# A linear-attention recurrence whose instruction order is a plan made in the kernel, on one core of a Trainium2

## The chip, the cores and the metric

The kernel runs on one core of a Trainium2 chip. The core has a matrix engine (TensorE, PE; its weight loads are listed apart as PEld), a vector engine (VectorE, DVE), an activation engine (ScalarE, ACT), a general engine (GpSimd, POOL) and SyncE (SP), which here only issues transfers (DMAs). Each engine takes its instructions strictly in the order in which they stand in its program and waits at each one until its inputs are there and its output buffer is free; the order of each engine is fixed when the kernel is built. The metric is the time of one execution in microseconds (us).

## The reference

Two parts follow each other: a recurrence over 768 time steps for 4 sequences of 8 heads with head size 40, and a mixture of 8 experts over its 3072 outputs.

```python
for t in range(S):
    y[:, :, t] = np.einsum('bhd,bhde->bhe', rt, state)
    Sa = np.einsum('bhde,bhe->bhd', state, at)
    state_decay = state * wt[:, :, None, :] - np.einsum('bhd,bhe->bhde', Sa, bt)
    state = state_decay + np.einsum('bhd,bhe->bhde', vt, kt)
...
logits = x @ w_gate
logits = logits - logits.max()
P = np.exp(logits)
for _ in range(8):
    P /= P.sum(1, keepdims=True) + 1e-09
    P /= P.sum(0, keepdims=True) + 1e-09
    P *= N / E
for e in range(E):
    h = np.maximum(x @ w1[e], 0.0)
    ye = h @ w2[e]
    out += P[:, e:e + 1] * ye
```

## The kernel before

The recurrence (function `attention`, lines 29 to 385) is cut into 12 chunks of 64 steps. Within a chunk the steps are solved as a triangular system, so that matrix products take the place of the loop over steps; between chunks a state of 40 by 40 per head is carried. A unit is one chunk of one sequence: 12 x 4 = 48 units, numbered chunk by chunk, and each unit holds 8 heads in 4 pairs.

Four kinds of work make up the recurrence.

- `prep(c, b)` needs only the inputs of unit (c, b). SP loads `inp`; VectorE scans the decays into q (L114), takes a reciprocal (L118) and scans g (L122); GpSimd (VectorE for the first units) multiplies kb and the two halves of ab (L133, L139, L140) and copies cc (L138); TensorE makes ll (L145) and the transposes kt (L153); VectorE masks ll into sx (L155), ScalarE copies the rest into sx and bb and stores lt to a DRAM buffer ld. What prep makes (sx, bb, g, cc) stays in one of 17 sets of buffers until the unit has been recurred, so preparations can run up to 17 units ahead.
- The inversion runs for two chunks at once, 128 small triangular blocks of 32 by 32, one in each partition. Eight transfers bring them from ld into lu (L342), 42 VectorE instructions build the inverse in un (L170 and L173 column by column, then products and reductions of 512, 1024 and 2048 elements, L179 and L182), one copy (L331) transposes it, and it goes out to the DRAM buffers ud and nd.
- `tload` and `tmat` read ud and nd back and join two blocks of 32 into a triangular factor tt of 64 (gp, L226, and op, L231, on TensorE, copies on ScalarE).
- `recur(c, b)` is the chain of a unit: av (L251), mask f (L252), two products xc (L259), copies x1 and c1 (L265, L266), pu with tt (L270), pm (L272), c2 (L277), ws (L279), then y (L281) to the DRAM buffer xd and z (L292), which, transposed by TensorE (zt, L297), feeds the next chunk of the same sequence. `gate` multiplies y with the gate weights (lp, L307), and a VectorE copy (L312) keeps the logits.

The order is made in two steps. The list `ev` gives each piece of work a time in arbitrary units, and sorting it gives the order in which the code emits instructions:

```python
t = max(t, t0 + P0 + PD * i) if s else -20 + 0.01 * i
ev.append((t, do_prep, (s,) + cb + (i == 0,)))
...
for i, (fn, a) in enumerate(INV):
    ev.append((t + INV_DT * i, fn, (us,) + a))
...
for _, fn, args in sorted(ev, key=lambda x: x[0]):
    fn(*args)
```

A list scheduler with a timing model of its own (`schedule_with_timeline_sim=True`) then takes instructions from that order as their inputs and buffers come free in its model, and so fixes each engine's program. PSUM is divided into three pools of 4, 2 and 2 banks (`ps`, `pq`, `pt`), by kind of product.

The expert part follows from L450 on. Its weights and inputs are prepared on all engines while the last units still run; its buffers lie over those of the recurrence. From block `N_MAN` on its order is written out by hand. The products are `p` (L545) and `op` (L610).

Of the kernel before, what the change touches and what calls it, by code (L numbers as in the profile page):

```python
# [28 lines left out]
def attention(ctx, tc, d, xd, ps, pq, pt, gs, lg):  # L29
# [5 lines left out]
    io = ctx.enter_context(tc.tile_pool(name="a_io", bufs=1))  # L35
    wk = ctx.enter_context(tc.tile_pool(name="a_wk", bufs=2))
    dr = ctx.enter_context(tc.tile_pool(name="a_dr", bufs=2, space=bass.MemoryType.DRAM))

    cst = const.tile([128, 64 + 64 + 104 + 128 + 40 + 260], F32, name="cst")
    nc.sync.dma_start(out=cst, in_=d["cst"])  # L40
# [6 lines left out]
    NTB = 2  # L47
    sx_b, bb_b, g_b, cc_b = ([None] * NSX for _ in range(4))
    raws = {}
    for n in range(NCH * NB - NSX, NCH * NB):  # L50
        i, pool = n % NSX, sets[n - NCH * NB + NSX]
        if i in IN_SETS or i in KB_SETS:
            raw = pool.tile([128, 1508], F32, name=f"st{i}")
            raws[i] = raw
            sx_b[i] = raw[0:R2, 0:832].rearrange("r (p h x) -> r p h x", h=2, x=104)
            bb_b[i] = raw[:, 832:1248].rearrange("r (p x) -> r p x", x=104)
            g_b[i] = raw[0:R2, 1248:1504].rearrange("r (p x) -> r p x", x=64)
            cc_b[i] = raw[0:R2, 1504:1508]
            continue
        sx_b[i] = pool.tile([R2, NP, 2, 104], F32, name=f"sx{i}")  # L60
        bb_b[i] = pool.tile([128, NP, 104], F32, name=f"bb{i}")
        g_b[i] = pool.tile([R2, NP, 64], F32, name=f"g{i}")
        cc_b[i] = pool.tile([R2, NP], F32, name=f"cc{i}")
    tt_b = [const.tile([128, 4 * NP, 128], F32, name=f"tt{i}") for i in range(NTB)]
    td_b = [const.tile([128, 4 * NP, 32], F32, name="td")]
    lg_b = [const.tile([128, 4 * NP, 64], F32, name="lg")]
    ab_b = [pin.tile([R2, NP, 128], F32, name=f"ab{i}") for i in range(2)]
    g1_b = [pin.tile([R2, NP, 64], F32, name=f"g1{i}") for i in range(1)]
    vz_b = [const.tile([R2, NP, 104], F32, name=f"vz{i}") for i in range(5)]
# [8 lines left out]
    for t in g1_b + ab_b:  # L78
        nc.vector.memset(t, 0.0)

    def clear():
        nc.gpsimd.memset(unf, 0.0)
        nc.gpsimd.memset(unf[:, 0:1024:33], 1.0)
        for t in vz_b + c1_b + lg_b:
# [725 lines left out]
```

## Time and profile before

| | us |
|---|---|
| median of 3 runs | 1890.27 |
| lowest and highest run | 1883.09, 1900.79 |
| the profiled execution | 1888.5 |
| its span, first to last instruction | 1886.7 |

The profile shows the profiled execution alone, and its mean granted TensorE clock is 0.945. A row of its groups reads: line, engine, operation, output and input tiles with their sizes, count, then busy time in us and mean duration in ns, then the idle time ahead of them and what ended it. A row of the answers on one line of code has the shortest, the median and the longest duration in ns, and the first and last start. "Records" are the entries of the trace: an fp32 matmul of the program leaves two, a transpose one. TensorE is busy for 94% of the span, VectorE for 74%, ScalarE for 45%, GpSimd for 48%; such shares run over stages with different limits, so the prediction looks at stages.

### The profile page before, as it was taken

The numbers are of one execution on the slowest core, as the hardware profiler recorded it, in microseconds if no ns is written. First come the engines' busy times: TensorE is split into PE (matmuls) and PEld (weight loads), VectorE is DVE, ScalarE is ACT, GpSimd is POOL, SyncE is SP. The second block draws the span as 40 slices with busy tenths as digits, with TensorE's granted clock in tenths as the row PEclk, the third lists the DMA queues.
The fourth block names the chain that finished last, engine by engine and source line by source line (L and its number), as shares of the span: only waits on it lengthen the run. The fifth ranks groups of instructions, "written<-read, shape, count | busy, mean of one in ns | idle before, by whom it ended". The sixth has DMA issues, their size and how long they took to land.

```text
span 1886.7 us, 31821 instructions
## 1 busy us (share of the span) xinstructions
PE 1768.5 (94%) x12035; PEld 1731.1 (92%) x12035; DVE 1395.1 (74%) x2330; ACT 853.9 (45%) x1845; POOL 896.9 (48%) x845
## 2 busy tenths in 40 slices
PE   4478989889998999999999999999999999999999
PEld 4368878789888999999999999999999999999999
DVE  7766768686579877776867777886776767777676
ACT  6346566655553444343433434345343433434342
POOL 6636457562345355371835628004461826537170
PEclk9568889988889999999999999999999999999999
DMA  8567777855732011110201102111110201111011
GB/s 192 102 131 160 137 156 144 176 128 102 164 96 70 32 43 37 37 61 14 73 26 49 55 19 74 55 33 38 37 55 19 73 19 56 37 37 57 17 37 42
DMA packets 187838, 136.26 MB, mean 72 GB/s; under 512 B 155941, under 2 KB 165285, under 8 KB 187685
## 3 DMA queue, kind: packets, MB, share of 16 engines
q1 hardware_dynamic: 184485, 128.98, 27.6%
q10 hardware_dynamic: 3200, 5.25, 1.1%
q8 instruction: 95, 1.56, 0.3%
q14 instruction: 58, 0.48, 0.1%
HBM read 113.74 MB, written 20.45 MB: 71 GB/s over the span
## 4 chain that ended last, share of the span: by engine, by line
PE 76%; DVE 10%; DMA 6%; issue 3%; POOL 2%; ACT 2%; SPq 1%; DVEq 0%; POOLq 0%; ACTq 0%
PE op L610 35%; PE p L545 32%; DMA inp<-in_inp_dram 2%; PE xc L259 2%; DVE pr L179 2%; PE pu L270 1%; PE av L251 1%; PE c L277 1%; DVE q L114 1%; PE ll L145 1%; PE lp L307 1%; PE gp L226 1%; DMA nd<-pr 1%; POOL ab L140 1%; DVE g L122 1%
## 5 line engine op out<-in xcount | busy, mean ns | idle before, releaser
L545 PE MATMUL p<-xch,wh 128*128 128x384 f32 (+1 forms) x1792 | 605.3, 339 | 5.2 <-DVE cs L654 1.8
L566 ACT ACTIVATE hh<-sm 128x384 fp32r<-128x384 f32 x512 | 269.5, 527 | 726.3 <-DVE sm L563 726.3
L610 PE MATMUL op<-wh,hh 128*128 128x320 f32 x1536 | 477.3, 311 | 1.0 <-ACT hh L566 0.9
L610 PE MATMUL op<-wl,hh 128*128 128x320 f32 x1536 | 474.7, 310 | 0.0
L610 PE MATMUL op<-wh,hl 128*128 128x320 f32 x1536 | 468.0, 310 | 4.4 <-DVE hl L569 4.4
L491 POOL TENSOR_TENSOR wl<-ws,wh 128x640 fp32r<-128x640 f32 x60 | 103.1, 1719 | 608.4 <-ACT wh L489 608.1
L569 DVE SCALAR_TENSOR_TENSOR hl<-sm,hh 128x384 fp32r<-128x384 f32 x512 | 370.8, 757 | 2.8 <-ACT hh L566 2.3
L545 PEld LDWEIGHTS p<-xch,wh 128*128 128x128 f32 (+1 forms) x1792 | 337.9, 189 | 8.4 <-DVE u L563 2.7
L545 PE MATMUL p<-xcl,wh 128*128 128x384 f32 x896 | 303.1, 338 | 0.0
L545 PE MATMUL p<-xch,wl 128*128 128x384 f32 x896 | 302.3, 337 | 0.0
L610 PEld LDWEIGHTS op<-wh,hh 128*128 128x128 f32 x1536 | 290.6, 189 | 1.7 <-ACT hh L566 1.5
L610 PEld LDWEIGHTS op<-wh,hl 128*128 128x128 f32 x1536 | 287.1, 188 | 5.4 <-DVE hl L569 5.3
L610 PEld LDWEIGHTS op<-wl,hh 128*128 128x128 f32 x1536 | 291.4, 190 | 0.0
L563 DVE TENSOR_TENSOR sm<-p,u 128x384 f32<-128x384 f32 x384 | 232.6, 615 | 9.2 <-PE p L545 0.4
L545 PEld LDWEIGHTS p<-xcl,wh 128*128 128x128 f32 x896 | 169.0, 189 | 0.0
L545 PEld LDWEIGHTS p<-xch,wl 128*128 128x128 f32 x896 | 169.0, 189 | 0.0
L563 DVE TENSOR_TENSOR sm<-p,p 128x384 f32<-128x384 f32 x128 | 71.3, 557 | 130.1 <-PE p L545 76.2
L563 DVE TENSOR_TENSOR p<-p,p 128x384 f32<-128x384 f32 x128 | 71.1, 555 | 101.5 <-PE p L545 101.0
L563 DVE TENSOR_TENSOR u<-p,p 128x384 f32<-128x384 f32 x128 | 70.8, 553 | 59.4 <-PE p L545 58.1
L145 PE MATMUL ll<-ab,kb 104*128 104x128 f32 x336 | 61.3, 340 | 50.6 <-POOL ab L140 22.2
L499 POOL TENSOR_TENSOR wl<-ss,wh 128x512 fp32r<-128x512 f32 x60 | 90.7, 1512 | 32.1 <-ACT wh L496 28.0
L145 PEld LDWEIGHTS ll<-ab,kb 104*128 104x128 f32 x336 | 53.2, 241 | 54.7 <-POOL ab L140 27.4
(161 smaller groups left out, 2845.0 us busy)
## 6 DMA issues: line engine op xcount, KB each, us to landing
ws<-in_wts_dram SPq DMA_DIRECT2D x60, 832.0 KB
inp<-in_inp_dram SPq DMA_DIRECT2D x42, 521.6 KB
rb<-in_r_dram SPq DMA_DIRECT2D x48, 208.0 KB
ld<-lt ACTq DMA_DIRECT2D x40, 128.0 KB
vz<-in_v_dram SPq DMA_DIRECT2D x48, 104.0 KB
f<-in_vt_dram SPq DMA_DIRECT2D x48, 80.0 KB
xd<-y SPq DMA_DIRECT2D x96, 40.0 KB
st<-in_inp_dram SPq DMA_DIRECT2D x6, 521.6 KB
```

The source lines that it names most:

```text
L114: nc.vector.tensor_tensor_scan(out=q.rearrange("r p t -> r (p t)"), data0=w65[:, 0:260], data1=one65, initial=0.0, op0=ALU.mult, op1=ALU.add)
L122: nc.vector.tensor_tensor_scan(out=g.rearrange("r p t -> r (p t)"), data0=w65[:, 260:516], data1=g1.rearrange("r p t -> r (p t)"), initial ...
L145: nc.tensor.matmul(ll[:, p], lhsT=kb[:, p], rhs=ab[:, p], start=True, stop=True)
L179: nc.vector.tensor_tensor(out=prv, in0=a.unsqueeze(2).broadcast_to([nu, n_c, n_r, n_k]), in1=m.rearrange("u k r -> u r k").unsqueeze(1).br ...
L259: nc.tensor.matmul(xc[h][:, p], lhsT=pp["sx"][:, p, h], rhs=f[:, p, h], start=True, stop=True)
L491: g.tensor_tensor(out=wl[:, 0:640], in0=raw[:, 256:896], in1=wh[:, 0:640], op=ALU.subtract)
L499: g.tensor_tensor(out=lv[:, 3:7], in0=so[:, :, 0], in1=hv[:, 3:7, 0], op=ALU.subtract)
L545: nc.tensor.matmul(o, lhsT=w_, rhs=x_, start=(j == 0), stop=(j == 3))
L563: eng.tensor_tensor(out=out, in0=x, in1=y, op=ALU.add)
L566: nc.scalar.activation(out=hh[:, f, h], in_=sm[f][:, h], func=AF.Relu)
L569: v.scalar_tensor_tensor(out=hl[:, f, h], in0=sm[f][:, h], scalar=0.0, in1=hh[:, f, h], op0=ALU.max, op1=ALU.subtract)
L610: nc.tensor.matmul(ops[i], lhsT=a[:, h, cs], rhs=w_[:, cw], start=(f == 0 and h == 0 and j == 0), stop=(last and h == 1 and j == 2))
```

## The change

The recurrence is written anew as operations of a class `Plan`. Each operation names its engine, a duration, what it depends on, a priority `key`, and which buffers and banks it takes and gives back. `Plan.layout` walks through planned time and gives each free engine the ready operation with the lowest key whose buffers are free; `Plan.emit` then issues everything in that order, and a `manual_schedule` for all five engines keeps it. What each operation computes stays the same; in the diff, code that only moved is left out.

```diff
+LAT = {"PE": 0.25, "DVE": 0.1, "ACT": 0.1, "POOL": 0.12, "SP": 1.9, "AQ": 1.9}
+class Plan:
...
+            for eng, lst in cand.items():
+                if busy.get(eng, 0.0) > now + 1e-9:
+                    continue
+                best = None
+                for o in lst:
+                    if best is not None and (o.key, o.n) >= (best.key, best.n):
+                        continue
...
+                    if any(len(self.free[p]) < k for p, k in need.items()):
+                        continue
+                    best = o
...
+    def emit(self):
+        for o in self.order:
+            o.fn()
...
-        nc.gpsimd.tensor_copy(out=cc, in_=q[:, :, 64])
+            (v_ if CC_DVE else g_).tensor_copy(out=st(cc_b), in_=q()[:, :, 64])
...
-            (nc.sync if cb < N_SP else nc.scalar).dma_start(out=ld[GRP[c][1], :, b], in_=lt)
+        o_ld = op("AQ", 0.08, lambda: a_.dma_start(out=ld[GRP[c][1], :, b], in_=lt()), [o_lt], key, (), rel_lt, xfer=0.5)
...
-        prv = prf[us, 0:n_c * n_r * n_k].rearrange("u (c r k) -> u c r k", r=n_r, k=n_k)
-        nc.vector.tensor_tensor(
-            out=prv, in0=a.unsqueeze(2).broadcast_to([nu, n_c, n_r, n_k]),
-            in1=m.rearrange("u k r -> u r k").unsqueeze(1).broadcast_to([nu, n_c, n_r, n_k]), op=ALU.mult)
-        nc.vector.tensor_reduce(out=dst, in_=prv, op=ALU.add, axis=AX.X)
+        prv = prf[us, 0:n_c * n_r * n_k].rearrange("u (c k r) -> u c k r", r=n_r, k=n_k)
+            v_.tensor_tensor(
+                out=prv, in0=a.unsqueeze(3).broadcast_to([nu, n_c, n_k, n_r]),
+                in1=m.unsqueeze(1).broadcast_to([nu, n_c, n_k, n_r]), op=ALU.mult)
+            v_.tensor_reduce(out=dst, in_=prv.rearrange("u c k r -> u c r k"), op=ALU.add, axis=AX.X)
...
-        (nc.vector if c >= 9 else nc.gpsimd).tensor_tensor(out=z, in0=ws[:, :, 64:104],
+        o_z = op("DVE" if Z_DVE else "POOL", 0.33 if Z_DVE else 0.45, lambda: (v_ if Z_DVE else g_).tensor_tensor(
...
+        k_inv = T_C * cs[0] - M_INV - (W_INV if s else 0.0)
+    for c in range(NCH):
+        for b in range(NB):
+            recur(c, b, T_C * (c + b / 4))
+    total = P.layout()
+    ctx.enter_context(tc.manual_schedule(engines={
...
+    P.emit()
...
+T_C = 32
+M_INV = 20
+W_INV = 40
...
-        ps, pq, pt = (actx.enter_context(tc.tile_pool(name=f"a_ps{i}", bufs=n, space=bass.MemoryType.PSUM))
-                      for i, n in enumerate((PC, PQ, PT)))
+        banks = [actx.enter_context(tc.tile_pool(name=f"a_ps{i}", bufs=1, space=bass.MemoryType.PSUM)).tile(
+            [128, 512], F32, name=f"bk{i}") for i in range(8)]
```

Besides the order, five things differ: the small copies cc go from GpSimd to VectorE (`CC_DVE`), the products z of chunks 9 and 10 from VectorE to GpSimd (`Z_DVE` is false), all 48 stores of ld go through ScalarE's queue (8 of them were on SP's), PSUM is one pool of eight banks, and in `contract` the product is laid out with r innermost, so that the reduction reads with a step. Line numbers after the change are others: q is L261, sx L327, f L536, pm L569, ws L579, the gate copy L600, the inversion L357 to L372 with its copy L426; on TensorE ll is L312, kt L324, av L533, xc L544, pu L565, c2 L576, lp L596, zt L617, gp L476, op L485.

The first place is on VectorE, between the first product of 2048 elements of the third inversion (pr from un and lu) and its next product. The number behind a name tells one buffer or tile from another. Before:

```order
L179 TENSOR_TENSOR pr_206<-un_204,lu_205 128x2048
L114 SCALAR_TENSOR_TENSOR q_2154<-inp_2152,cst_144 104x260
L312 COPY lg_62<-lp_2102 64x8
L252 TENSOR_TENSOR f_2122<-av_2126,cst_144 104x8x64
L182 TENSOR_REDUCE gt_207<-pr_206 128x128
L312 COPY lg_62<-lp_2193 64x8
L118 RECIPROCAL g10_196<-q_2154 104x4
L155 TENSOR_TENSOR st10_186<-ll_2075,cst_144 64x8x64
L279 TENSOR_TENSOR ws_2144<-c2_2139,c11_203 104x416
L272 TENSOR_TENSOR pm_2187<-pu_2182,cst_144 128x416
L179 TENSOR_TENSOR pr_206<-un_204,lu_205 128x1024
```

And after the change (bk is a PSUM bank):

```order
L368 TENSOR_TENSOR pr_222<-un_220,lu_221 128x2048
L327 TENSOR_TENSOR st10_175<-bk2_77,cst_164 64x8x64
L372 TENSOR_REDUCE gt_223<-pr_222 128x128
L600 COPY lg_62<-bk1_73 64x8
L368 TENSOR_TENSOR pr_222<-un_220,lu_221 128x1024
```

Of eight instructions of units and preparations between the two products two are left; the steps of an inversion stand closer together, and the units that stood among them follow after its end.

The second place is TensorE at the end of the third inversion. Before, from the first row that is not needed by an instruction of that inversion's stretch on VectorE:

```order
L259 MATMUL xc0_2393<-f_2326,st15_147 104x104 x4
L259 MATMUL xc1_2394<-f_2326,st15_147 104x104 x4
L251 MATMUL av_2431<-rb_2425,vz1_198 104x128 x4
L297 MATMUL zt_2459<-cst_144,z_2354 40x104 x4
L277 MATMUL c2_2466<-pm_2391,st14_146 104x104 x4
L270 MATMUL pu_2521<-x1_2409,tt1_191 128x104 x4
L259 MATMUL xc0_2559<-f_2427,st16_148 104x104 x4
L259 MATMUL xc1_2560<-f_2427,st16_148 104x104 x4
```

After:

```order
L617 MATMUL bk3_81<-cst_164,z0_216 40x104 x4
L544 MATMUL bk6_93<-f0_203,st4_169 104x104 x4
L544 MATMUL bk4_85<-f0_203,st4_169 104x104 x4
L565 MATMUL bk1_73<-x11_207,tt1_183 128x104 x4
L533 MATMUL bk3_81<-rb0_201,vz4_198 104x128 x4
L576 MATMUL bk5_89<-pm1_209,st4_169 104x104 x4
L324 MATMUL bk6_93<-cst_164,kb0_192 128x104 x4
L544 MATMUL bk4_85<-f1_204,st5_170 104x104 x4
L312 MATMUL bk0_69<-ab1_187,kb0_192 128x128 x4
L544 MATMUL bk1_73<-f1_204,st5_170 104x104 x4
```

The kinds of rows are the same; what moved is how many of them follow before the next inversion: 224 records before, 412 after, with the products of preparations (L312, L324) among them.

The third place is VectorE ahead of the second inversion. Before:

```order
L331 COPY pr_206<-un_204 128x1024
L118 RECIPROCAL g10_196<-q_892 104x4
L122 SCALAR_TENSOR_TENSOR st16_148<-inp_890,g10_196 104x256
L155 TENSOR_TENSOR st15_147<-ll_794,cst_144 64x8x64
L155 TENSOR_TENSOR st16_148<-ll_906,cst_144 64x8x64
L114 SCALAR_TENSOR_TENSOR q_986<-inp_984,cst_144 104x260
L118 RECIPROCAL g10_196<-q_986 104x4
L114 SCALAR_TENSOR_TENSOR q_1070<-inp_1068,cst_144 104x260
L170 TENSOR_TENSOR pr_206<-un_204,lu_205 128x4
```

After:

```order
L579 TENSOR_TENSOR ws0_210<-bk3_81,c10_199 104x416
L283 COPY st1_166<-q0_191 104x4
L261 SCALAR_TENSOR_TENSOR q0_191<-inp1_190,cst_164 104x260
L569 TENSOR_TENSOR pm1_209<-bk2_77,cst_164 128x416
L266 RECIPROCAL g10_188<-q0_191 104x4
L270 SCALAR_TENSOR_TENSOR st2_167<-inp1_190,g10_188 104x256
L600 COPY lg_62<-bk1_73 64x8
L283 COPY st2_167<-q0_191 104x4
L536 TENSOR_TENSOR f1_204<-bk4_85,cst_164 104x8x64
L357 TENSOR_TENSOR pr_222<-un_220,lu_221 128x4
```

Before, the second inversion (L170 with 4 elements) came after two more preparations and ahead of any pm; after, four pm and three ws of the first chunk stand ahead of it.

771 lines of the change are left out of this document (471 added, 300 removed).

## The prediction

> **What bounds the kernel now.** I read the page's slices first, to see where time can go at all. Times are us from the span's start, one slice is 47.2 us.
>
> ```profile
> PE   4478989889998999999999999999999999999999
> PEclk9568889988889999999999999999999999999999
> DMA  8567777855732011110201102111110201111011
> ```
>
> From slice 13 on (about 610 us) TensorE is full at full clock; that is the expert part, whose code the change leaves alone. Only the recurrence, about 560 us, can gain or lose. Its ends come from the answers on two lines (first and last start at the end of each):
>
> ```profile
> L270 PE MATMUL pu<-x,tt x384: 255/275/542, 117.8 to 556.1; 128*128 128x104 f32 x192
> L312 DVE COPY lg<-lp x48: 123/158/160, 143.9 to 561.8; 64x8 f32<-64x8 f32 x48
> ```
>
> The last gate copy starts at 561.8: call the end 562. Next I looked for the six inversions on VectorE (L170 to L331) in its timeline and cut the recurrence at their starts and ends. The busy time of each engine in these stages is the view that carries the sum (columns: stage, then length, busy us and instructions of PE, PEld, DVE, ACT, POOL, then granted clock, DMA share, GB/s).
>
> ```profile
> 56.60:100.80 44.20, 13.81 (x60) 12.24 (x60) 40.32 (x55) 13.57 (x34) 30.96 (x22) 0.50 0.47 95
> 100.80:118.80 18.00, 11.46 (x76) 10.72 (x77) 4.11 (x8) 6.78 (x18) 5.89 (x9) 0.50 1.01 175
> 118.80:163.20 44.40, 39.29 (x367) 36.63 (x366) 43.66 (x63) 26.31 (x66) 26.36 (x23) 0.92 0.56 123
> 163.20:207.60 44.40, 42.89 (x343) 40.30 (x342) 18.12 (x34) 28.16 (x72) 18.51 (x29) 0.79 0.88 161
> 207.60:260.50 52.90, 46.09 (x410) 42.61 (x408) 50.38 (x75) 32.99 (x83) 31.32 (x30) 0.90 0.62 133
> 260.50:284.80 24.30, 22.26 (x188) 21.02 (x188) 11.08 (x21) 15.34 (x40) 10.99 (x16) 0.79 0.84 180
> 284.80:338.50 53.70, 48.13 (x456) 44.47 (x454) 49.67 (x77) 35.16 (x89) 37.47 (x33) 0.97 0.73 147
> 338.50:362.40 23.90, 21.50 (x226) 20.11 (x226) 11.56 (x22) 17.20 (x44) 14.13 (x20) 1.00 0.84 177
> 362.40:421.50 59.10, 51.35 (x414) 47.85 (x413) 50.29 (x75) 33.59 (x84) 30.17 (x29) 0.83 0.66 135
> 421.50:441.70 20.20, 18.63 (x156) 17.72 (x155) 6.74 (x14) 12.07 (x30) 6.42 (x10) 0.75 0.67 136
> 441.70:485.00 43.30, 41.02 (x400) 38.35 (x398) 39.30 (x57) 22.95 (x58) 7.76 (x10) 0.93 0.40 88
> 485.00:562.00 77.00, 73.54 (x627) 68.71 (x627) 43.44 (x79) 42.95 (x97) 33.02 (x36) 0.82 0.58 146
> ```
>
> While an inversion runs, VectorE is 85 to 98% busy and sets the pace; TensorE meanwhile still gets through 367 to 456 records. Between inversions VectorE is 33 to 48% busy and TensorE over 88%, at 7.7 records per us where its clock is 0.75 to 0.79 (343/44.4, 188/24.3, 156/20.2), 8.1 in the last stage (627/77) and 9.5 at full clock (226/23.9). So two kinds of stage alternate, and a new order is costed by how it splits the work between them.
>
> **The change, part by part.** *The inversion.* The product now walks memory in the order in which the matrix lies, and the reduction takes the strided walk instead. Its rows, and rows for both kinds of walk elsewhere:
>
> ```profile
> L179 DVE TENSOR_TENSOR pr<-un,lu 128x2048 f32<-128x2048 f32 x6 | 22.6, 3773 | 0.1
> L179 DVE TENSOR_TENSOR pr<-un,lu 128x1024 f32<-128x1024 f32 x6 | 11.5, 1918 | 0.0
> L179 DVE TENSOR_TENSOR pr<-gt,un 128x512 f32<-128x512 f32 x12 | 12.8, 1064 | 0.1
> L182 DVE TENSOR_REDUCE gt<-pr 128x128 f32<-128x2048 f32 x6 | 13.7, 2283 | 0.0
> L521 DVE TENSOR_TENSOR xt<-xs,xt x9: 410/417/425, 521.3 to 1256.2; 128x256 f32<-128x256 f32 x9
> L133 DVE TENSOR_TENSOR st<-st,q 104x512 f32<-104x512 f32 x1 | 0.7, 661 | 0.0
> L649 DVE TENSOR_REDUCE cl<-pmat 128x8 f32<-128x192 f32 x8 | 4.2, 526 | 0.2
> L645 DVE TENSOR_REDUCE rs<-pmat 128x24 f32<-128x192 f32 x8 | 2.8, 348 | 0.2
> L331 DVE COPY pr<-un x6: 1018/1029/1291, 99.8 to 483.7; 128x1024 f32<-128x1024 f32 x6
> ```
>
> One inversion has two products of 2048, two of 1024 and four of 512 elements, 8192 in all: 2 x 3.77 + 2 x 1.92 + 4 x 1.06 = 15.6 us. An unstrided product of two SBUF operands takes 0.417 us at 256 and 0.661 at 512, 0.95 ns an element: 2 x 2.12 + 2 x 1.15 + 4 x 0.66 = 9.2 us, a saving of 6.4. L649 reduces 192 elements in steps of 32 bytes, L645 the same 192 side by side: 526 against 348 ns, 0.93 ns an element. On 8192 elements that gives back 7.6 us; the product's own surcharge for its stride, (3.77 - 2.12)/2048 = 0.81 ns, would give back 6.6. I take 6.9: the inversion costs 0.5 us more. Ends: 6.4 less (the stride free for a reduction) and 1.2 more, nearer to the second, as L649 is the same operation with the same step. The Trainium skill states the mechanism in "SBUF — State Buffer", section "Door 1: The DMA port swizzle": lines of 16 bytes, with a penalty for each access that crosses to a new line. By that rule both walks pay, and the two rows agree. Its page "VectorE: DVE Perf Modes", section "Mode 1× (REGULAR)", says instead one result a cycle with any stride; by that the change saves the whole 6.4 per inversion. The rows decide for the first.
>
> *VectorE's order.* Counted in the order, the third to fifth inversions hold five or six q, five sx, five f, six pm, five ws and six gate copies before; after, they hold 2 q, 3 sx, 2 f, 2 pm, 3 ws and 3 gate copies. Durations:
>
> ```profile
> L252 DVE TENSOR_TENSOR f<-av,cst 104x512 f32<-104x512 f32 x48 | 32.6, 679 | 18.5 <-PE av L251 17.7 <-DMA td<-ud 0.5
> L279 DVE TENSOR_TENSOR ws<-c,c 104x416 f32<-104x416 f32 x48 | 27.9, 582 | 19.9 <-PE c L277 17.6 <-ACT st L142 0.9 <-ACT vz L300 0.5
> L272 DVE TENSOR_TENSOR pm<-pu,cst 128x416 f32<-128x416 f32 x48 | 27.8, 579 | 8.7 <-PE pu L270 8.7
> L155 DVE TENSOR_TENSOR sx<-ll,cst x27: 653/676/686, 14.0 to 386.1; 64x512 f32<-64x512 f32 x27
> L114 DVE TENSOR_TENSOR_SCAN q<-inp,cst x42: 669/699/1224, 24.7 to 419.3; 104x260 f32<-104x260 f32 x42
> L122 DVE TENSOR_TENSOR_SCAN st<-inp,g x21: 654/685/1700, 48.1 to 423.9; 104x256 f32<-104x256 f32 x21
> L118 DVE RECIPROCAL g<-q 104x4 f32<-104x4 f32 x48 | 8.4, 176 | 0.7
> ```
>
> From the 53.7 us of the fourth inversion go 4 of q, reciprocal and g (4 x 1.56 = 6.2), 2 sx (1.4), 3 f (2.0), 4 pm (2.3), 2 ws (1.2) and 3 copies (0.5); the copy of cc, now on VectorE, adds 0.3 (priced as the gate copy, 0.16) and the inversion 0.5. Result 40.9, three times. In the same way the first goes from 44.2 to 36.7, the second from 44.4 to 35.0 (it loses 4 f, 4 pm, 3 ws, 2 preparations), the sixth from 43.3 to 39.2. From the second on: 35.0 + 3 x 40.9 + 39.2 = 197.
>
> *TensorE's order.* What left those stages must be done between them. From the order, with two records for an fp32 matmul and one for a transpose, TensorE has 412 records in each of the three stages that follow an inversion, then 328, then 664 in the last: 2228, where before it had 300, 224, 224, 184 and 612. During the inversions only 168 to 252 are left for it. At the 9.5 of the full-clock stage the first four take 1564/9.5 = 165 us; the last, with the expert preparation beside it, I put between 8.1 and 9.5, at 8.6: 77 us. Together 242, against 189.9 before (44.4 + 24.3 + 23.9 + 20.2 + 77.0).
>
> *The start.* The first inversion starts at 56.6 as before (eleven scans q stand ahead of it in both orders). It ends at 93; the triangular factor then needs the 17 us that lie between 100.8 and the first pu at 117.8: 110. Before, the second inversion began right there; after, four pm, three ws and seven preparations stand first. That is three more units; the fastest 20 us windows of L270 hold 24 records, three units, so at 6.7 us each it begins at about 130. At 10 us each, as in the first windows, it would be 140.
>
> ```profile
> 120.00:140.00 20.00, 2.11 (x16) 1.95 (x16) 0.91 0.42 95
> ...
> 320.00:340.00 20.00, 3.17 (x24) 2.92 (x24) 1.00 0.84 172
> ```
>
> *Parts that end in nothing.* Eight stores of ld move from SP's queue to ScalarE's: each waits only for the copy ahead of it on the same engine; if ScalarE were the bound it would cost an issue each (0.5 us on SP, 4 us in all). Eight z move from VectorE to GpSimd, 8 x 0.45 us beside y; GpSimd is at most 51% busy in the last four stages (30.17 of 59.1), which covers them, and without that cover they are 4 us. One pool of eight banks in place of 4, 2 and 2 can end the wait that the old pools show, and no more. The rows of these three parts (issue on SP, z on GpSimd, the wait):
>
> ```profile
> 24.57 0.53 SPq L148 DMA_DIRECT2D ld<-st  x1
> ...
> L292 POOL TENSOR_TENSOR z<-ws,cc x20: 445/452/3972, 129.5 to 470.2; 104x160 f32<-104x160 f32 x20
> ...
> PE xc L259 <- DVE lg L312: 7.1, 4, 2.9
> ```
>
> Here "waited for, us in total, times, longest" follow each other: 7 us in four times at most, inside TensorE's stages; it stands in their rate. If the cover fails, its end is 0.
>
> *The sum.* 130 + 197 + 242 = 569 against 562: +7. The profiled execution took 1888.5 (1.8 below the median 1890.27): 1888.5 + 7 = 1896, rounded.
>
> **Rivals.** *The stride is free for a reduction.* For it: the copy L331 reads the same matrix across its rows and takes 1.03 us for 1024 elements, 1 ns each. Against: L649. Six inversions lose 6.9 each, 41 us: 1855.
>
> *TensorE runs the dense stages without a gap.* Busy time alone in the full-clock stage gives 226/21.5 = 10.5 records per us; 2228/10.5 = 212, 30 less: 1866. For it: preparations run further ahead and banks are shared, so waits fall. Against: no stage before reached it.
>
> *Slower: the clock falls while VectorE has the stage.* With 168 to 252 records in 35 to 41 us TensorE is half idle during each inversion, as in the first stage above (13.8 of 44.2 busy), where the granted clock was 0.50. If the stage after it then runs like the three at 0.75 to 0.79, 7.7 per us in all five, it is 2228/7.7 = 289, 47 more: 1943; with 8.1 it is 275: 1929. It decides (1% slower) from a mean rate below 8.8. For it: three of five such stages ran so. Against: those were also waiting for inputs (DMA share 0.84 and more), and the stage at 0.84 with clock 1.00 shows that it need not. The Trainium skill's page "TensorE: Matmul & The Clock Gate", section "Why this matters for your kernels", tells to leave no idle gap above about 3 us or the clock halves; by that this rival would be the rule, and the row at 0.50 agrees with it.
>
> **How the numbers follow.** Forecast (1880 to 1912): 0.45. Free stride: 0.20. Gapless TensorE: 0.13. Slower by the clock: 0.22. About 1% (19 us) is what a measurement of this kernel can tell from no change. Faster than that (below 1871): 0.17 of the free stride, 0.08 of the gapless, 0.05 of the forecast, together 0.30. Slower (above 1909): 0.20 of the clock, 0.08 of the forecast, 0.28. Within: 0.42. The range takes the free stride to 1850 and the clock rival at 8.1 to 1928 and leaves some 0.2 out.
>
> **What would show it.** Right: L372 near 3.9 us at 2048 elements and L368 near 2.1; VectorE over 90% busy and TensorE under 65% while an inversion runs; stages of some 44 us after it with VectorE at 55%. Wrong: L372 at 2.3; a rate between inversions away from 9; a first pu far from 110; or an expert part that starts late, since its tiles lie over the buffers of other units than before, which I count as nothing.

## The result and the profile after

The changed kernel takes 1960.66 us (median of 4 runs, 1954.51 to 1965.28), the kernel before 1886.68 beside it: 1.0371 times as long, 95% interval 1.0328 to 1.0414. The forecast was 1896, the range 1850 to 1928. The profiled execution took 1965.28, its span is 1963.3.

The two rows of the page on TensorE, one slice being 49.1 us:

```profile
PE   4457979797997899999999999999999999999999
PEclk9557868686977899999999999999999999999999
```

Counted from 0, as in the prediction, TensorE is full from slice 14 on (about 690 us), before from slice 13 (about 610). What grew is the alternation ahead of it, 9 and 7 in turn, with the granted clock at 8 and 6. The stages, cut as before at the first row of each inversion, its copy (now L426) and the last gate copy (L600), with the same columns:

```profile
0.00:68.44 68.44, 36.12 (x187) 32.10 (x188) 44.55 (x82) 33.09 (x79) 30.20 (x42) 0.90 0.76 164
68.44:112.23 43.79, 8.62 (x35) 6.77 (x33) 37.32 (x45) 9.06 (x22) 7.36 (x10) 0.50 0.20 52
112.23:156.27 44.04, 36.85 (x296) 34.42 (x297) 23.95 (x45) 24.50 (x64) 22.53 (x29) 0.68 0.82 145
156.27:194.94 38.67, 25.28 (x180) 22.96 (x179) 37.58 (x46) 15.20 (x40) 9.05 (x10) 0.65 0.43 102
194.94:239.44 44.50, 43.50 (x387) 41.50 (x386) 27.67 (x52) 30.16 (x75) 22.24 (x28) 0.81 0.84 160
239.44:287.24 47.80, 37.77 (x261) 34.70 (x259) 40.19 (x53) 20.00 (x53) 11.93 (x13) 0.64 0.48 106
287.24:332.00 44.76, 41.97 (x382) 40.02 (x383) 28.36 (x52) 30.17 (x75) 22.58 (x28) 0.85 0.80 157
332.00:383.00 51.00, 38.50 (x261) 35.44 (x259) 39.76 (x53) 19.99 (x53) 11.63 (x13) 0.67 0.44 101
383.00:427.37 44.37, 41.66 (x382) 39.88 (x383) 27.64 (x52) 30.16 (x75) 22.26 (x28) 0.85 0.83 161
427.37:474.45 47.08, 34.62 (x258) 31.90 (x257) 40.30 (x53) 19.99 (x53) 11.94 (x13) 0.72 0.49 108
474.45:510.35 35.90, 33.74 (x315) 32.16 (x314) 17.43 (x35) 22.65 (x58) 12.62 (x17) 0.85 0.69 127
510.35:546.66 36.31, 31.44 (x271) 29.09 (x270) 35.40 (x46) 15.74 (x41) 7.57 (x8) 0.81 0.39 86
546.66:631.43 84.77, 75.35 (x644) 71.36 (x643) 40.59 (x68) 45.29 (x103) 36.58 (x45) 0.78 0.54 135
```

The recurrence ends at 631.4 instead of 561.9. Of these 69.5 us, 17.5 are lost by the first pu, which starts at 135.3 instead of 117.8, and 52 behind it. Read a pair of rows as one period of two chunks: from the third inversion to the fourth it is 92.6 us (before 77.2), and the pair holds 643 records. TensorE was busy for 79.7 us of it at clocks of 0.64 and 0.85: 37.8 x 0.64 + 42.0 x 0.85 = 60 us of work at full clock. Before, with 598 records, it was 46.1 x 0.90 + 22.3 x 0.79 = 59. The work is the same. Of the 15.4 us more, 11.4 are the same work at a lower clock (79.7 us busy, before 68.4) and 4 are gaps (12.8 us, before 8.8).

The gaps have names. In the view of waits, from the second inversion to the end of the recurrence (waited for, us in total, times, longest), the changed kernel has

```profile
PE bk L576 <- DVE pm L569: 16.1, 8, 4.3
PE bk L565 <- ACT x L555: 14.2, 13, 2.9
...
DVE ws L579 <- PE bk L576: 35.2, 24, 2.5
DVE pm L569 <- PE bk L565: 35.0, 23, 3.7
```

and the kernel before, over its same stages,

```profile
PE c L277 <- ACT c L266: 3.1, 2, 1.7
...
DVE ws L279 <- PE c L277: 17.6, 15, 4.6
DVE pm L272 <- PE pu L270: 8.7, 9, 1.8
```

These are the steps of one unit: xc, x, pu, pm, c2, ws. Each engine now stands waiting for the other at steps that before had other units' work between them. Most of TensorE's gaps lie in the inversions: by the busy times above it is idle for 53.3 us in the second to sixth, of 71.3 in all from the second on. VectorE's waits for pu and c2 lie between the inversions instead: inside them pm never waits and ws for 7.2 us.

A gap can cost more than itself. Windows of 1 us of the changed kernel, same columns:

```profile
242.00:243.00 1.00, 0.73 (x7) 0.52 (x5) 0.91 (x3) 0.94 (x4) 0.00 (x0) 1.00 1.08 169
243.00:244.00 1.00, 0.17 (x1) 0.17 (x2) 0.95 (x3) 0.95 (x3) 0.00 (x0) 1.00 1.08 200
246.00:247.00 1.00, 1.00 (x18) 1.00 (x17) 0.96 (x2) 0.72 (x2) 0.00 (x0) 0.65 0.80 175
250.00:251.00 1.00, 1.00 (x11) 0.98 (x10) 0.46 (x2) 0.94 (x4) 0.00 (x0) 0.50 0.51 79
256.00:257.00 1.00, 1.00 (x9) 1.00 (x9) 0.90 (x3) 0.00 (x0) 0.49 (x1) 0.73 0.44 162
```

TensorE idles 1.1 us up to 243.8, the clock falls to one half at 246.3 and is back at 256.5, though TensorE was busy throughout in between; the records per us go from 18 to 11. From the first inversion's end to the last gate copy the clock is at one half for 257 us, before for 132 (summed over windows of 0.5 us). The falls are as many, 16 and 15 after the start, and all but one of the 16 (before all but two) have 0.7 us or more of idle time in the 3.4 us ahead of them. A spell lasts 14 us in the mean and 7 before. Further gaps fall into the longest (12 us into one of 44, 6 into one of 24), but spells without any gap also last up to 13.7 us.

### The profile page after: what moved, and what is told of

It is laid out like the page before. It is cut to its first block, busy times and chain, and to the rows that moved or that the text cites. A ratio compares the mean times of both kernels' runs of the same rounds, so it can differ in the third digit from the quotient of the medians.

```text
span 1963.3 us, 31696 instructions
## 1 busy us (share of the span) xinstructions
PE 1798.2 (92%) x12035; PEld 1759.8 (90%) x12035; DVE 1433.2 (73%) x2369; ACT 852.1 (43%) x1845; POOL 838.2 (43%) x806
## 4 chain that ended last, share of the span: by engine, by line
PE 70%; DVE 4%; issue 1%; ACT 0%; POOL 0%; DMA 0%; SPq 0%; DVEq 0%; ACTq 0%; POOLq 0%
PE op L868 34%; PE p L803 31%; PE bk L544 1%; PE bk L565 1%; PE bk L576 1%; PE bk L533 1%; DVE sm L821 1%; PE bk L596 0%; DVE hl L827 0%; DVE xch L791 0%; DVE u L821 0%; DVE pr L368 0%; PE bk L617 0%; DVE xcl L789 0%; PE bk L485 0%
## 5 line engine op out<-in xcount | busy, mean ns | idle before, releaser
L821 DVE TENSOR_TENSOR sm<-p,p 128x384 f32<-128x384 f32 x128 | 71.3, 557 | 128.8 <-PE p L803 73.7
L544 PE MATMUL bk<-f,st 104*104 104x104 f32 x768 | 111.3, 308 | 14.7 <-ACT st L305 7.3
L277 POOL TENSOR_TENSOR kb<-inp,q 104x512 f32<-104x512 f32 x40 | 48.7, 1218 | 168.2 <-issue 47.6
L544 PEld LDWEIGHTS bk<-f,st 104*104 104x104 f32 x768 | 102.8, 220 | 17.3 <-ACT st L342 6.1
L583 POOL TENSOR_TENSOR y<-ws,st 104x256 f32<-104x256 f32 x48 | 41.6, 867 | 174.4 <-DVE ws L579 131.1
```

The lines of the kernel that those rows point to most:

```text
L277: o_kb = op("POOL", 1.18, lambda: g_.tensor_tensor(out=kb(), in0=inp()[:, 516:1028].rearrange("r (p k t) -> r p k t", p=NP, k=2), in1=q()[ ...
L544: nc.tensor.matmul(xc[:, p], lhsT=st(sx_b)[:, p, h], rhs=f_b[r_f.slot][:, p, h], start=True, stop=True)
L583: o_y = op("POOL", 0.73, lambda: g_.tensor_tensor(out=y_b[r_y.slot], in0=ws()[:, :, 0:64], in1=st(g_b), op=ALU.mult), [o_ws], key + 8 * K1 ...
L821: eng.tensor_tensor(out=out, in0=x, in1=y, op=ALU.add)
```

## The experiments

Each ratio is to the kernel before, run beside it on the same chip, with its 95% interval. In the table, spacing is the median number, over the units of chunks 1 to 10, of TensorE's records, in its order, between the end of a unit's xc and its pu, and between its pu and its c2. Split is the number of records in the third to fifth inversions, and between them. Gaps are TensorE's idle time from the second inversion to the last gate copy, half clock as above; these and the first pu, in us, are from the profiled execution.

| run | spacing | split | first pu | gaps, us | half clock, us | recurrence ends | ratio |
|---|---|---|---|---|---|---|---|
| before | 38, 46 | 416 / 224 | 117.8 | 38.5 | 132 | 561.9 | 1 |
| after | 20, 18 | 228 / 412 | 135.3 | 71.3 | 257 | 631.4 | 1.0371 (1.0328 to 1.0414) |
| after_list | 24, 32 | 372-408 / 240-268 | 119.9 | 49.1 | 185 | 584.8 | 1.0151 (1.0112 to 1.0189) |
| after_dur | 12, 16 | 356 / 284 | 135.2 | 60.1 | 242 | 630.5 | 1.0398 (1.0338 to 1.0457) |
| after_far | 40, 38 | 204-260 / 396-416 | 124.6 | 87.8 | 218 | 621.0 | 1.0372 (1.0328 to 1.0415) |
| after_spread | 12, 16 | 388-400 / 220-244 | 134.7 | 69.7 | 240 | 639.4 | 1.0438 (1.0405 to 1.0470) |
| after_both | 28, 28 | 388-416 / 224-232 | 132.3 | 59.1 | 181 | 593.8 | 1.0252 (1.0202 to 1.0302) |
| after_both2 | 32, 36 | 368-412 / 220-240 | 130.5 | 72.1 | 205 | 610.2 | 1.0295 (1.0264 to 1.0326) |
| before_near | 16, 26 | 360-372 / 268-288 | 121.3 | 71.0 | 237 | 638.4 | 1.0361 (1.0336 to 1.0386) |
| before_far | 46, 56 | 432-438 / 208 | 120.2 | 46.3 | 157 | 573.4 | 1.0037 (1.0020 to 1.0054) |

**The single edits.** First the stores of ld, back on SP in the changed kernel:

```diff
-        o_ld = op("AQ", 0.08, lambda: a_.dma_start(out=ld[GRP[c][1], :, b], in_=lt()), ...
+        o_ld = op("AQ", 0.08, lambda: (nc.sync if n < 8 else a_).dma_start(out=ld[GRP[c][1], :, b], in_=lt()), ...
```

> The first eight stores of ld go through SP's queue again; the order of TensorE, VectorE and GpSimd is the changed kernel's, word for word. If ScalarE's wait at its first store (10.3 us, 13.6 to 23.9 us) delays the preparations, the first inversion begins 5 to 10 us earlier than 68.4 and the run takes 1950 to 1955 us. If TensorE's own wait for the load of vz at 23.9 us holds them anyway, nothing moves: 1960.

1956.02 us, ratio 1.0372 (1.0330 to 1.0413) beside 1.0371 without the edit: nothing gained that can be measured, though in the profile the first inversion begins at 64.9 instead of 68.4. The reverse, in the kernel before:

```diff
-N_SP = 8
+N_SP = 0
```

> The kernel before with all stores of ld on ScalarE's queue, as in the changed kernel; TensorE's order stays word for word, VectorE's but for one row. If a store on ScalarE holds that engine until an earlier load has landed, the first inversion begins 5 to 10 us later than 56.6 us and the run takes 1892 to 1897 us. If the store is free there, as the prediction had it, 1887.

1897.29 us, 1.0046 (1.0015 to 1.0077): a small loss, about as expected, the first inversion at 62.2 instead of 56.6. The layout of the inversion alone, in the kernel before (the hunk on `contract` of the change):

> The kernel before with the new layout of the inversion's products alone. By the prediction six inversions cost 0.5 us more each: 1890 to 1893. By the durations in the changed kernel's trace (products 58.4 and reductions 93.3 us against 93.2 and 57.9) it is no change, 1887 to 1890. If the reduction's stride were free, 1850.

1888.73 us, 1.0002 (0.9974 to 1.0029): no change, as the durations say. The copies of cc and the products z alone:

```diff
-        nc.gpsimd.tensor_copy(out=cc, in_=q[:, :, 64])
+        nc.vector.tensor_copy(out=cc, in_=q[:, :, 64])
...
-        (nc.vector if c >= 9 else nc.gpsimd).tensor_tensor(out=z, ...
+        nc.gpsimd.tensor_tensor(out=z, ...
```

> The kernel before with the copies of cc on VectorE and all products z on GpSimd, as in the changed kernel, and nothing else: split and spacing stay (400 to 432 records in the inversions, 37 and 52 records). The changed kernel's 48 copies took 17.7 us of VectorE, 0.37 each instead of the 0.16 of the prediction. If they are part of the rest, half of them in the inversions, where VectorE sets the pace: 1895 to 1903 us. If nothing waits for them, 1885 to 1893.

1898.16 us, 1.0041 (1.0019 to 1.0064). The rows on L138 sum to 17.1 us for 48 copies; which part of the loss is theirs and which the products', this run doesn't separate. The pool of eight banks alone:

```diff
-        ps, pq, pt = (actx.enter_context(tc.tile_pool(name=f"a_ps{i}", bufs=n, space=bass.MemoryType.PSUM))
-                      for i, n in enumerate((PC, PQ, PT)))
+        ps = pq = pt = actx.enter_context(tc.tile_pool(name="a_ps", bufs=8, space=bass.MemoryType.PSUM))
```

> The kernel before with one pool of eight PSUM banks, taken in turn, instead of 4, 2 and 2. The list scheduler answers with another split: 116 to 160 records in the third to fifth inversions and 460 to 536 between (before 416 and 224), at spacings of 44 and 52 (before 38 and 46). If the split alone costs, as in the run with longer latencies, 1930 to 1960 us. If a long spacing makes up for it, or the free banks do, 1885 to 1900.

2155.05 us, 1.1416 (1.1376 to 1.1457), worse than either theory had it. Its waits show another thing than was meant: TensorE waits 170 us, in 33 times, for ab ahead of ll. The likely reason is that banks taken in turn pull the products of preparations forward to where their input isn't there; it was not tried. The plan of the changed kernel takes any free bank, so this run doesn't tell what its pool costs.

**The order, given back to the list scheduler.**

```diff
-    ctx.enter_context(tc.manual_schedule(engines={
-        mybir.EngineType.PE, mybir.EngineType.DVE, mybir.EngineType.Activation, mybir.EngineType.Pool,
-        mybir.EngineType.SP}))
     P.emit()
```

> The changed kernel without the manual schedule in the recurrence: the list scheduler may again take instructions from the order in which the plan issues them; all other edits stay (one pool of eight banks, cc on VectorE, z on GpSimd, all stores of ld through ScalarE, the new layout of the inversion). In its order the third to fifth inversions hold 372 to 408 TensorE records, the changed kernel's 228, the kernel's before 416. If the fixed order costs the time, the recurrence ends near 575 us and the run takes 1890 to 1910 us. If the other edits cost it, whatever the order (the copies of cc take 17.7 us of VectorE in the changed kernel's trace), it stays above 1940.

1917.41 us: some 43 of the 74 us come back with every other edit kept. In the profile the recurrence ends 46.6 us earlier: 15.4 are won by the first pu (119.9, before the change 117.8), with preparations again among the steps of the first inversion, and 31 behind it. The third inversion and the stretch behind it, in its profile:

```profile
221.42:274.79 53.37, 47.06 (x389) 43.67 (x388) 48.35 (x73) 31.27 (x77) 28.22 (x23) 0.83 0.61 133
274.79:304.61 29.82, 25.73 (x260) 23.99 (x259) 14.54 (x31) 18.67 (x50) 12.70 (x18) 0.94 0.90 163
```

The period is 83.2 us for 649 records. With the stores back on SP as well:

> The changed kernel under the list scheduler, with the first eight stores of ld on SP's queue as before: the two causes found so far taken back together, the layout of the inversion, the one pool of banks, cc on VectorE and z on GpSimd kept. The list scheduler alone gave 1917, the stores cost the kernel before 0.46%. If these two explain the loss but for the 5 us that the expert part starts later, 1900 to 1910. If the kept edits cost 20 us, 1917 as without the stores.

1933.90 us, 1.0222 (1.0197 to 1.0247): a miss, slower instead of faster. The half clock is 214 us, 29 more than without the edit. The list scheduler answered the edit with another order of TensorE, so eight stores on another queue shift the time by 0.7% the wrong way, and the 0.46% above is no fixed price of the stores.

**The plan's durations, spacing and split.** True durations first (`PE_SLOW` multiplies TensorE's):

```diff
-            out.append((0.15 + n * 1.04e-3, partial(contract, us, dst, a, m, 1), False))
+            out.append((0.15 + n * 1.80e-3, partial(contract, us, dst, a, m, 1), False))
...
+PE_SLOW = 1.3
```

> The plan with two durations nearer to the trace: the inversion's reductions at 1.80 instead of 1.04 ns an element (3832/2048 = 1.87 measured) and every TensorE product 1.3 times as long. The inversions from the third on then hold 356 records instead of 228. If the thin TensorE work in the inversions costs the time, the recurrence ends some 20 us earlier and the run takes about 1935 to 1945 us. If the fixed order as such costs it (VectorE waits in order for late products), it stays within 10 us of 1960.

1959.77 us: no change. The split is halfway to that of before, but the spacings are shorter still. Then the spacing alone:

```diff
-LAT = {"PE": 0.25, "DVE": 0.1, "ACT": 0.1, "POOL": 0.12, "SP": 1.9, "AQ": 1.9}
+LAT = {"PE": 1.75, "DVE": 1.6, "ACT": 1.6, "POOL": 1.62, "SP": 1.9, "AQ": 1.9}
```

> Two rivals stand against each other. In TensorE's order of the changed kernel the median unit has 20 records between the end of its xc and its pu and 18 between its pu and its c2; before, 38 and 46. One theory: steps of one unit stand too close together, so that each engine in its fixed order waits for the other, and every gap on TensorE brings 3 to 4 us of halved clock. The other: the split of the records between the inversions and the stretches between them (412 and 228 in the changed kernel, 224 and 416 before). Here the plan's latencies between engines are 1.5 us longer and nothing else is changed: the spacings become 40 and 38, the split stays 396 to 416 and 204 to 260. If the spacing decides, TensorE's gaps from the second inversion on fall from 71 to under 50 us, and the run takes 1905 to 1930 us. If the split decides, 1955 to 1970.

1958.64 us, no change: the spacing alone is not it. In its profile the first pu comes 10.7 us earlier, but TensorE's gaps grow to 87.8 us. The split (the durations above, `PE_SLOW = 1.6`, `M_INV = 12`, `W_INV = 52`):

> The reverse of the run with longer latencies: the plan with TensorE's products 1.6 times as long, the reductions at 1.80 ns an element, and the inversions' keys 8 later and spread over 52 instead of 40. The split becomes 212 to 244 records between inversions and 384 to 400 in them, as before the change; the spacings become 12 and 16 records, still closer than in the changed kernel. If the spacing decides, 1950 to 1980 us. If the split decides, 1890 to 1915.

1971.35 us, a little slower. The split is that of before, but the spacings fell to 12 and 16, below the changed kernel's, so this run and the one with true durations don't test the split by itself. Both together (latencies 1.0 us longer, `PE_SLOW = 1.3`, `M_INV = 12`, `W_INV = 52`):

> Both at once: latencies 1.0 us longer, products 1.3 times as long, reductions at 1.80 ns, the inversions' keys as in the run with the split of before: 388 to 452 records in inversions, 208 to 276 between, spacings 28 and 28. If spacing and split each carry a part, this is the fastest plan: 1890 to 1915 us. If spacing alone decides, by its 28 records it stands between the changed kernel and the run with 40: 1925 to 1945. If the fixed order as such costs the time, 1955.

1934.89 us: 1.0252 against 1.0371, intervals apart. A third of the loss comes back in this plan, the only one so far with both numbers mended, and half clock falls to 181 us. Farther in the same direction (latencies 1.5 us longer, `M_INV = 10`, `W_INV = 54`):

> As the run with both, with latencies 1.5 instead of 1.0 us longer and the inversions' keys two later: spacings 32 and 36 (before 38 and 46), split 368 to 412 records in the third to fifth inversions and 220 to 336 between. If spacing and split together carry the loss, it comes nearer to before than the run with both (1.0252): 1905 to 1925 us. If something else in the change holds the rest, it stays at 1930 to 1940.

1945.34 us, 1.0295: no better, a miss. So the two numbers don't describe a good order fully.

**The loss made in the kernel before.** None of the change's edits, only the times at which the steps of a unit are emitted:

```diff
-                ev.append((5 * c + k + SKEW * b, step, (c, b)))
+                ev.append((5 * c + 1.25 * b + STEP * k, step, (c, b)))
...
-SKEW = 1.1
+SKEW = 1.25
+STEP = 0.5
```

> The kernel before, with its list scheduler and every other edit of the change left out, but with the five steps of a unit emitted half as far apart in the list of events (0.5 instead of 1 unit of time, the units 1.25 apart): the spacings fall from 38 and 46 records to 16 and 26, the split is 356 to 372 in inversions and 268 to 308 between. If the spacing decides, the kernel before loses what the changed one lost, with none of its edits: 1930 to 1960 us. If another edit of the change is behind it, 1885 to 1900.

1957.74 us, 1.0361: as much as the whole loss. It is not the same loss in every part: the first pu starts at 121.3, 3.5 us later than before, and all the rest, 73 us, comes behind it, where the changed kernel loses 52. Its period looks like the changed kernel's, 96.1 us for 686 records:

```profile
215.11:270.81 55.70, 48.67 (x358) 45.90 (x358) 46.89 (x66) 27.46 (x70) 25.72 (x25) 0.70 0.53 110
270.81:311.17 40.36, 37.13 (x328) 34.93 (x326) 18.11 (x31) 26.36 (x67) 18.36 (x25) 0.86 0.79 169
```

And the other way, with `STEP = 1.2` (in this order a set is refilled ahead of its last reader, so some values are those of another unit; the instructions are the same in kind and number):

> The kernel before with the steps of a unit farther apart in its list of events (1.2 instead of 1.0, the units 1.25 instead of 1.1): spacings 46 and 56 records instead of 38 and 46, split 432 to 438 in the inversions and 192 to 214 between. If more spacing still removes gaps, 1870 to 1885 us. If before has enough of it, 1885 to 1895; if the few buffers between the steps (two of x1, pm, ws) bind, 1895 to 1910.

1897.61 us, 1.0037 (1.0020 to 1.0054): more spacing gives nothing more.

**The gaps or the clock.** Idle products in the gaps of the changed kernel, its order kept:

```diff
+    def fill(r):
+        for _ in range(N_FILL if in_inv[0] else 0):
+            nc.tensor.matmul(banks[r.slot][0:128, 0:104], lhsT=ident, rhs=mask_p, start=True, stop=True)
...
             pu = bank(b_pu, 128, 416, "r (p x) -> r p x", p=NP)
+            fill(b_pu)
```

> The changed kernel, its order kept, with four idle products (128x104, of constants, into the bank that the next real product overwrites) ahead of each ll, first xc, pu, c2 and lp that TensorE reaches while an inversion runs: 260 products more, each 0.27 us at full clock, 70 us of TensorE work that computes nothing. In the changed kernel the granted clock is at one half for 257 us between the first inversion's end and the last gate copy, against 133 us in the kernel before, and each fall follows a gap on TensorE of 1 to 4 us. If the gaps and the halved clock behind them cost the time, more work makes it faster: less than 200 us at half clock, the recurrence ends near 600 us, 1925 to 1945 us. If VectorE's waits in a fixed order cost it whatever the clock, the added work comes on top where it isn't hidden: 1965 to 2000.

1969.15 us, 1.0415 (1.0382 to 1.0448): not faster. But the stages moved. The third inversion and the stretch behind it:

```profile
237.66:288.32 50.66, 44.63 (x365) 42.39 (x363) 40.10 (x53) 19.99 (x53) 11.79 (x13) 0.83 0.45 101
288.32:332.38 44.06, 38.92 (x383) 36.95 (x383) 26.91 (x52) 30.06 (x75) 21.52 (x28) 0.92 0.87 166
```

Half clock fell from 257 to 154 us. The four stretches between inversions, which hold no idle product, sum to 158.8 us instead of 169.5; the five inversions, which hold them, to 229.2 instead of 220.9. So the halved clock carries some 11 us of those stretches; the inversions became 8 us longer with the added work in them. With fewer, and none ahead of pu and c2:

> Idle products again in the changed kernel's order, three instead of four, and only ahead of ll, the first xc and lp, not of pu and c2, for which VectorE waits: 120 products, 32 us of TensorE work at full clock, in the inversions alone. In the first such run the stretches between inversions, in which no idle product stood, ran 169.5 - 158.8 = 10.8 us shorter at a granted clock of 0.92 to 1.00, while the inversions took 8 us longer. If the halved clock carries a part of the loss, the stretches between are shorter again and the inversions no longer: 1940 to 1952 us. If it does not, 1958 to 1975.

1959.56 us, 1.0371 (1.0336 to 1.0405), half clock 178 us: 32 us of added work cost nothing that can be measured, and gained nothing. The size of the clock's own share stays open. In the kernel before, two idle products ahead of every pu:

> The kernel before with two idle products of constants ahead of every pu, into its own tile: 96 products, 26 us of TensorE work at full clock. If the halved clock (133 us of the recurrence) is set off by gaps like the one in which TensorE waits for the copy of xc ahead of pu, part of it goes and the time falls to 1870 to 1885. If the gaps lie elsewhere, or cost nothing, the work comes on top: 1895 to 1915.

1910.69 us, 1.0105 (1.0074 to 1.0137): most of the 26 us of added work came on top. Gaps fell from 38.5 to 31.7 us, half clock did not (142 us).

## Why the prediction was wrong

The sum put the end of the recurrence at 569; it came at 631.4. The start is 26 us of the difference, the inversions 24, the stretches between them 12, and the expert part adds 7 that were counted as nothing. In each of the first three terms the sum moved work from stage to stage at paces taken from the order before, and put what the new order does to waits and to the clock at nothing.

*The inversion's price was right.* It was to rise by 0.5 us, with a strided reduction as dear as a strided product:

```profile
L372 DVE TENSOR_REDUCE un<-pr 128x128 f32<-128x2048 f32 x6 | 23.0, 3832 | 0.1
L372 DVE TENSOR_REDUCE gt<-pr 128x128 f32<-128x2048 f32 x6 | 21.4, 3570 | 0.1
L283 DVE COPY st<-q 104x4 f32<-104x4 f32 x48 | 17.7, 368 | 0.0
L368 DVE TENSOR_TENSOR pr<-gt,un 128x2048 f32<-128x2048 f32 x6 | 13.7, 2286 | 0.0
```

Forecast for 2048 elements were 3.9 us for the reduction and 2.1 for the product, measured are 3.6 to 3.8 and 2.3; over all six inversions products fell from 93.2 to 58.4 us and reductions rose from 57.9 to 93.3, 0.1 us more per inversion. The rival with a free stride is out: the same reduction took 2.28 us without a stride. The Trainium skill's page "VectorE: DVE Perf Modes", section "Mode 1× (REGULAR)", doesn't hold here as it was read, a stride without a price. The Trainium skill's page "SBUF — State Buffer", section "Door 1: The DMA port swizzle", with its penalty for each new line of 16 bytes, agrees with these rows. The copies of cc, priced at 0.16 us, took 0.37 in the mean (L283 above).

*"VectorE over 90% busy while an inversion runs" failed.* In the third to fifth it is busy 78 to 86%, and TensorE, forecast under 65%, 74 to 79%. The sum gave 197 us from the second inversion on; it is 220.9. The 197 were made from the lengths of the stages before, less the rows that move out, so 16.8 us of those stages' idle time were in them and 180 us of VectorE's work. Measured are 193.2 of work and 27.6 idle: 13 and 11 us more. The idle time has names, here in the fourth inversion:

```profile
DVE lg L600 <- PE bk L596: 6.1, 1, 6.1
DVE ws L579 <- PE bk L576: 2.3, 1, 2.3
DVE st L327 <- ACT lt L316: 2.0, 1, 2.0
```

Over the five inversions the gate copy waits 11.1 us for its product lp, ws 7.2 for c2, and sx 4.4 for ScalarE's copy lt. The longest of these waits shows how a small row holds up a large block:

```profile
340.00 3.30 PE L476 MATMUL bk<-td,lg 64*64 64x32 f32 x29
...
345.67 1.02 PE L596 MATMUL bk<-gs,y 104*64 104x8 f32 x8
...
346.73 0.16 DVE L600 COPY lg<-bk 64x8 f32<-64x8 f32 x1 [6.07 <-PE bk L596]
```

The copy, 0.16 us of work, stands ahead of the inversion's next product in VectorE's order, and its own product stands behind the products of gp and op in TensorE's, at half clock (338.5 to 352.1). A product of eight records takes 2.0 us there instead of 1.1. The added work is in part known: rows of VectorE that follow each other overlap in the trace (in the fourth inversion they sum to 53.9 us in 49.7 busy before, 41.9 in 39.8 after), so a row that moves out frees less than its mean duration, and two copies of cc took 1.4 us in each of the third to fifth instead of 0.3. This is the step of the sum that failed in the inversions: work moved out of a stage was counted, what VectorE would then wait for in a fixed order was not.

*The rate between inversions was sized too high.* 2110 records were seen there in 254.3 us, 8.3 per us; with the 2228 counted in the order it is 8.8, against 9.2 in the sum: 12 us more than forecast. The 9.5 of the first four stretches came from the one stage before that ran at full clock; the clock now stands at 0.78 to 0.85. That is the mechanism of the rival on the clock, just at the 8.8 that it named as its bound, and the run with idle products gave back 11 us of it. It carries 12 of the 62 us, and its 1929 to 1943 left the other two terms as forecast. The Trainium skill's page "TensorE: Matmul & The Clock Gate", section "Why this matters for your kernels", tells to leave no gap above about 3 us; the trace agrees in kind, but here the clock fell after gaps of 1 to 2 us (1.1 us up to 243.8).

*The start was 26 us late (156.3 instead of 130).* The first inversion begins at 68.4 instead of 56.6 (12 us), lasts 43.8 instead of 36.4 (7), and the first pu follows its end after 23 us instead of 17 (6). From the first pu to the second inversion it is 21 us, 20 in the sum: the price of the three units was right.

Two things that were counted at nothing are seen in it. The stores of ld on ScalarE's queue were to wait "only for the copy ahead of it". In the timeline of the changed kernel:

```profile
12.98 0.60 ACT L316 ACTIVATE st<-bk 64x512 f32<-64x512 f32 x1 [0.34 <-PE bk L312]
23.89 0.49 ACTq L319 DMA_DIRECT2D ld<-st  x1
24.41 0.42 ACT L339 COPY st<-bk 64x320 f32<-64x320 f32 x1 [10.83 <-DMA vz<-in_v_dram]
```

The copy ends at 13.6, the store goes out at 23.9, and ScalarE stands for 10.3 us. In the compiled program all transfers share eight semaphores in turn, so this store also waits for the load of vz eight transfers ahead of it, which lands then. By the run with these stores on SP this is worth 3.5 of the 12 us; the rest was not tried. And from 83 to 114 us TensorE has nothing at all:

```profile
111.20 1.03 DVE L426 COPY pr<-un 128x1024 f32<-128x1024 f32 x1
112.15 0.69 DVE L261 TENSOR_TENSOR_SCAN q<-inp,cst 104x260 f32<-104x260 f32 x1
...
113.07 1.18 POOL L277 TENSOR_TENSOR kb<-inp,q 104x512 f32<-104x512 f32 x1 [32.35 <-DVE g L266]
...
114.31 0.95 PE L324 MATMUL bk<-cst,kb 104*128 104x104 f32 x4 [31.45 <-POOL kb L277]
```

TensorE waits for kb, kb for the scan q, and the scan stands behind the inversion's last row (L426) in VectorE's order, where it runs without a wait. Before, preparations stood among the first inversion's steps to its end, and under the list scheduler they do so again. SP's queue adds little to this hole:

```profile
SPq L416 <- DVE pr L368: 18.6, 1, 18.6
```

SP stands 18.6 us (81 to 99.9) at a load of the second inversion, whose buffer the first one still reads. The inputs of the next two scans had been asked for by then; the first scan that waits for an input queued behind it, at 123.2, waits 3.1 us.

*The expert part* was counted as nothing and takes 1331.9 us after the recurrence instead of 1324.8. Its first product begins 4.5 us ahead of the last gate copy (626.9), before 25.8 us ahead (536.1); what held it was not tried.

*What is shown.* The order carries the larger part: the list scheduler takes back 2.2 of the 3.7 points with all other edits kept, a third of it by the first pu and the rest behind it. An order alone can cost as much as the change did: steps set closer cost the kernel before 3.6 points with none of the other edits. That both come to nearly the same figure proves nothing by itself, as they lose it in different parts. The path behind the first pu, gaps on TensorE and the half clock after them, is argued and not shown. Over the runs of the table the end of the recurrence rises with the half clock, from 562 us at 132 to 638 at 237, and is 621 to 639 from 218 to 257; but idle products took some 80 to 100 us of half clock out of the changed kernel without making it faster. Not settled is the rest: the stores, and cc with z, cost 0.4 to 0.5 points each when tried in the kernel before, but mending the stores gained nothing twice, and the plan with spacing and split mended keeps 2.5. No run here beat the kernel before.

## What to carry to other kernels

When an order is made by a plan, count not only how much work each stage holds but what each engine will wait for in its fixed order: how many instructions of other work stand between a product and the step that needs it, and which large block stands behind a small step that waits. Compare these with the order that runs well, and test the plan against a list scheduler on the same edits. No single number settles it: here more spacing at the same split gained nothing, and spacing and split together a third of the loss. Cost the start by itself: work that could run beside the first long block, but is ordered behind it, leaves the other engines empty (31 us of TensorE here). A transfer moved to another engine's queue is priced by what it waits for there (10.3 us of ScalarE, of which 3.5 reached the first inversion).

## What the runs showed of the hardware

- In these traces the granted clock is one half or full, and its spells at one half last 3.4 us or a multiple of it (3.4, 6.8, 10.2, 13.7, 17.1). It can take 10 us of unbroken work to come back: in the kernel before, from 273.9 to 284.1 us, with TensorE busy throughout.
- A fall can follow a short gap: 1.1 us of idle time up to 243.8 in the changed kernel, then one half from 246.3 to 256.5.
- A VectorE copy of four elements per partition takes 0.14 us or up to 1.36 us, 0.37 in the mean of 48 (L283). The same copies on VectorE in the kernel before took 0.36 each in the mean of 48 (L138 of the run with cc moved); the cause was not tried.
